# Chunked attention and a feed-forward layer on one core: eight zero products in the front's waits, and the second batch's first keys loaded and interleaved at other steps

## The chip, the cores and the metric

The kernel runs on one core of one Trainium2 chip. The metric is the device time of one execution in microseconds (us), given as a median over runs; the profile is one further execution with the hardware profiler on. TensorE (PE) multiplies, VectorE (DVE), ScalarE (ACT) and GpSimd (POOL) do the rest, and transfers (DMAs) are issued from the queues of SyncE (SP) and GpSimd. PEld stands for TensorE's weight loads, which overlap its products. The granted clock (PEclk) is the share of its full clock that TensorE was given.

## The reference

Four batches, 8 heads of width 64, 768 tokens, eight memory keys and values a head. Each chunk of 32 queries sees the memory, 16 keys to the left of the chunk, the chunk, and 8 to the right; then comes a normalised feed-forward layer with a residual:

```python
for c in range(nc):                      # 24 chunks of 32
    l_start = max(0, c * 32 - 16); r_end = min(S, c * 32 + 32 + 8)
    q_c = q[:, :, c * 32 : c * 32 + 32]
    k_full = np.concatenate([mem_k, k[:, :, l_start:r_end]], axis=2)
    v_full = np.concatenate([mem_v, v[:, :, l_start:r_end]], axis=2)
    scores = scale * np.matmul(q_c, k_full.transpose(0, 1, 3, 2))
    a = softmax(scores)
    out[:, :, c * 32 : c * 32 + 32] = np.matmul(a, v_full)
x = out.transpose(0, 2, 1, 3).reshape(B, S, H * D)
xn = (x - mu) / np.sqrt(var + 1e-06) * g_ln
return x + np.maximum(xn @ w_ch1, 0.0) @ w_ch2      # 512 -> 2048 -> 512
```

## The kernel before

The 3072 tokens are 24 tiles of 128, six to a batch. A tile's attention is: scores (`qk`, products at line 316), their maximum and difference on VectorE (lines 325 and 328), the exponential on ScalarE (line 338), the weights turned through TensorE and copied (`pt`, lines 348 and 353), the product with the values (`val`, line 362), division and row sum on VectorE (`tokens`, lines 371 to 378), and the subtraction of the mean (`shift`, on ScalarE at line 389 for the first tiles and on GpSimd at line 385 later). `turn_x` turns the result through TensorE (line 414) and copies it (line 420). `root` squares it on ScalarE (line 400) and takes the power on GpSimd (lines 404 and 408).

The feed-forward layer works on pairs of tiles, `u` from 0 to 11. `up` makes two blocks of 128 hidden columns (line 452) and `relu` copies them (line 443). From pair 1 on `down7` makes the way back as seven block products instead of eight (line 528), from sums of blocks made on VectorE (`r_sum` line 522, `w2_sum` line 507), and adds each product to the residual (line 535).

Keys and queries of a batch come in two halves. `load_octets` issues two DMAs for a half from GpSimd's queue (line 111). For batch 0 `turn_k`, `turn_q` and `turn_v` turn them as they land (products at line 214, copies at lines 227 and 235). For later batches `mix` first copies a half into another order, two heads beside each other (line 246, on VectorE for the keys, on ScalarE for the queries), and `later_k` and `later_q` turn that (line 255). The values of later batches come head by head, two DMAs each (`load_v_head`, lines 120 and 125), also from GpSimd's queue, and `v_shared` copies shared rows within on-chip memory (line 142).

The order on each engine is the order of the program text: the schedule is written by hand, and each engine works through its queue strictly in that order, an instruction that waits holding all behind it. There are two parts.

- The front (to line 817) is a straight list of calls: the first tiles' attention, the first pairs, and the loads of both weight matrices. `warm(n, p)` (line 595) puts n products of 128x512 zeros on TensorE (line 599); their result goes to a bank that is overwritten later. The front uses them where TensorE waits for a transfer or a copy.
- From `u = 2` on a table `plan` says which calls are made at which of a pair's 17 steps: `at(u, step, fn, ...)` appends to a step's list; at even steps `up` follows the list, at odd steps `down7` of the pair before. Calls of one step run in the order in which they were entered.

For batch 2 (`b = 2`, so `u0 = 3`) the first halves of keys and queries belong to pair-step `w = 2`, which has steps of its own: keys loaded at step 5, queries at step 9, keys interleaved at step 10. At the same pair-step the table has, in this order, V loads at steps 0, 2 and 4, `qk` of tiles 6 and 7 at step 4, `val` of tile 6 at step 9, `val` of tile 7 at step 11, `turn_x` of tile 6 and `qk` of tile 8 at step 12, `root` of tile 6 at step 13, `turn_x` of tile 7 at step 14, and `qk` of tile 9 at step 15. `later_k` of the first half comes at step 1 of pair-step 3.

Of the kernel before, what the change touches and what calls it, by code (L numbers as in the profile page):

```python
# [16 lines left out]
def kernel(  # L17
# [43 lines left out]
    V = [sb.tile([128, NG, H, VW], FP16, name=f"V{i}") for i in range(2)]  # L61
# [26 lines left out]
    def slot():  # L88
        banks["turn"] += 1
        return banks["list"][banks["turn"] % len(banks["list"])]  # L90

    def use(*b):
        banks["list"], banks["turn"] = list(b), -1
# [4 lines left out]
    def free(ap, off, pattern, parts=None):  # L98

        p = list(ap.ap[0]) if parts is None else [ap.ap[0][0], parts]  # L100
        return bass.AP(tensor=ap.tensor, offset=ap.offset + off, ap=[p] + [list(x) for x in pattern])
# [103 lines left out]
    def copy_on(engine):  # L205
        return nc.scalar.copy if engine == "A" else nc.vector.tensor_copy

    def turn(src, jj, n, p=None):

        p = slot() if p is None else p  # L210
        pv = as16(p)
        for r in range(8):
            for par in range(2):
                nc.tensor.matmul(
                    out=pv[64 * par : 64 * par + 64, 2 * n * r : 2 * n * r + 2 * n],
                    lhsT=src[0 : 2 * n, 2 * jj + par, r, :],
                    rhs=identity[0 : 2 * n, 0 : 2 * n],
                    is_transpose=True, start=True, stop=True,
                    tile_position=(0, 64 * par),
                )  # L220
        return pv
# [10 lines left out]
    def to_rows(b, pv, jj, engine, n, oct0, lo=0, hi=None):  # L232

        hi = n if hi is None else hi
        copy_on(engine)(
            out=free(QD[b % 2], 2 * jj * S + 8 * (oct0 + lo), [[S, 2], [8, hi - lo], [1, 8]]),
            in_=free(pv, 2 * lo, [[1, 2], [2, hi - lo], [2 * n, 8]]),
        )
# [29 lines left out]
    def turn_k(b, half, jj, engine):  # L268
        to_stream(KT[b % 2], turn(raw[0][half], jj, 48), jj, engine, 48, 48 * half)
# [35 lines left out]
    def qk_products(t, p=None):  # L305
        b, tt = t // 6, t % 6
        p = slot() if p is None else p
        for y in range(2):
            for j in range(4):
                for gg in range(2):  # L310
                    g = 2 * tt + gg
                    for par in range(2):
                        rows, col = slice(64 * par, 64 * par + 64), 64 * gg + 32 * par
                        q0 = 64 * g + 32 * y
                        k0 = BLK * g + 32 * y
                        nc.tensor.matmul(  # L316
                            out=p[col : col + 32, 128 * j + 64 * y : 128 * j + 64 * y + 64],
                            lhsT=QD[b % 2][rows, j, q0 : q0 + 32],
                            rhs=KT[b % 2][rows, j, k0 : k0 + 64],
                            start=True, stop=True, tile_position=(64 * par, col),  # L320
                        )
        return p.rearrange("p (c k) -> p c k", c=8)

    def row_max(t, scores):
        nc.vector.tensor_reduce(out=nmx[t % 2], in_=scores, axis=AX.X, op=ALU.max)  # L325

    def less_max(t, scores):
        nc.vector.tensor_tensor(  # L328
            out=sub[t % 2].rearrange("p (c k) -> p c k", c=8), in0=scores,
            in1=free(nmx[t % 2], 0, [[1, 8], [0, 64]]), op=ALU.subtract,  # L330
        )

    def below_max(t, scores):
        row_max(t, scores)
        less_max(t, scores)
# [260 lines left out]
    def warm(n, p=upb[1]):  # L596

        for _ in range(n):
            nc.tensor.matmul(  # L599
                out=p, lhsT=zeros[:, 0:128], rhs=zeros, start=True, stop=True,  # L600
            )
# [29 lines left out]
    idle = two[:, 512:1024]  # L631
# [7 lines left out]
    nc.vector.memset(VT[:, :, KC - 8 : KC], 0.0)  # L639
    nc.vector.memset(V[0][0:16, 0, :, 64:VW], 0.0)  # L640
    nc.vector.memset(mhalf, -0.5)
    warm(4, idle)
    for j in range(2):
        turn_k(0, 0, j, "VA"[j])
    warm(1, idle)
    q0 = [turn(raw[1][0], j, 32, one[j]) for j in range(2)]
    for lo in (0, 16):
        for j in range(2):
            to_rows(0, q0[j], j, "VA"[j], 32, 0, lo, lo + 16)
    s0 = qk_products(0, two[:, 0:512])  # L650
    s1 = qk_products(1, dnb[0])
    below_max(0, s0)
    use(upb[0], upb[1])
    turn_v(0, 0, "A")
    weights(0)
    turn_v(0, 1, "V")
    row_max(1, s1)
    warm(2, idle)
    use(dnb[1], one[0], upb[0], upb[1])
    v_turn(0, "V")  # L660
    v_turn(1, "V")
# [159 lines left out]
    def at(u, step, fn, *args):  # L821
        plan.setdefault((u, step), []).append((fn, args))
# [33 lines left out]
    for b in range(2, B):  # L856
        u0 = 3 * b - 3
        for half in range(2):
            w = u0 - 1 + half
            at(w, 5 if w == 2 else 1, load_octets, 0, half, k, b, 48 * half, 48)  # L860
            at(w, 9 if w == 2 else 3, load_octets, 1, half, q, b, 48 * half, 48)
            at(w, 10 if w == 2 else 12, mix, 0, half, "V")
            at(w + 1, 5, mix, 1, half, "A")
            for n, step in enumerate((1, 6, 11, 15)):
                if n < 2:
                    at(w + 1, step, later_k, b, half, n, "V")
                else:
                    at(w + 1, step, later_q, b, half, n - 2, "A")
            for n, step in enumerate((0, 2, 4, 12, 13, 14, 15, 16)):
                at(w, step, load_v_head, b, 4 * half + n // 2, n % 2)  # L870
        at(u0 + 1, 0, load_v_ends, b)
        at(u0 + 1, 6, v_shared, b, 0, NG)
        at(u0 + 1, 6, v_mem, b)
        at(u0, 14, mem_cols, KT[b % 2], memKT[:, 4 * b : 4 * b + 4, :], True)
# [58 lines left out]
```

## Time and profile before

| what | us |
|---|---|
| median of 3 runs (lowest, highest) | 232.98 (232.91, 233.85) |
| the profiled execution | 233.83 |
| its span | 232.1 |
| TensorE busy in the span | 218.9 (94%) |
| VectorE busy | 162.8 (70%) |
| ScalarE busy | 124.6 (54%) |
| GpSimd busy | 115.6 (50%) |

The page of the profile gives each engine's busy time and the span in 40 slices of 5.8 us, in tenths. A row of instructions in order of time has: start, duration, engine, line, operation, output <- inputs, shape, count (xN when several were merged), and in brackets the idle time ahead of it and what ended it. A row of the chain of work has start, duration, and what the end of the execution hung on at that time. Matmuls are pipelined, so records of neighbouring products overlap a little, and the duration of one includes the time until its result stands.

### The profile page before, as it was taken

What the parts mean: (1) busy time and instruction counts of PE and PEld (TensorE: products, weight loads), DVE (VectorE), ACT (ScalarE), POOL (GpSimd) and SP (SyncE); (2) the same over time, 40 slices, a digit from 0 to 9 for tenths busy, and PEclk for the clock granted to TensorE, in tenths of its full rate; (3) what the DMA queues carried; (4) which work ended last, traced back from release to release, by engine and by line L of the source; (5) the groups of instructions that cost most, each with busy time, mean ns of one, the idle gap of its engine ahead of it and who ended that gap; (6) DMA issues with size and microseconds to landing.
All of it is one profiled execution on the core that took longest, in us unless ns stands there. A gap on an engine that the chain in (4) does not pass through costs nothing.

```text
span 232.1 us, 8538 instructions
## 1 busy us (share of the span) xinstructions
PE 218.9 (94%) x3712; PEld 190.6 (82%) x3712; DVE 162.8 (70%) x380; ACT 124.6 (54%) x237; POOL 115.6 (50%) x197
## 2 busy tenths in 40 slices
PE   7699987999998799999999999999999999999993
PEld 3556876876896789999989998999999999899982
DVE  4657665588995997797577796895684875646372
ACT  2243673979461748739646458558437265444310
POOL 7869998589943595912724945613031121220000
PEclk9959999999999999999999999999999999999999
DMA  5999999999898399783781991943102002011022
GB/s 79 189 205 205 215 213 200 187 76 60 76 176 120 101 76 143 123 98 45 141 114 14 151 160 51 111 81 76 45 6 85 8 3 90 3 48 45 1 93 92
DMA packets 43282, 23.25 MB, mean 100 GB/s; under 512 B 29884, under 2 KB 39676, under 8 KB 43172
## 3 DMA queue, kind: packets, MB, share of 16 engines
q0 software_dynamic: 38320, 14.48, 52.1%
q1 hardware_dynamic: 4924, 8.22, 12.6%
q8 instruction: 29, 0.48, 0.8%
q14 instruction: 9, 0.07, 0.1%
HBM read 29.02 MB, written 6.29 MB: 152 GB/s over the span
## 4 chain that ended last, share of the span: by engine, by line
PE 81%; DMA 6%; DVE 4%; POOL 3%; issue 2%; ACT 2%; POOLq 0%; DVEq 0%
PE upb L452 32%; PE dnb L528 26%; PE two L362 3%; DMA raw<-in_k_dram 3%; PE one L255 3%; PE dnb L477 3%; PE one L414 3%; DMA raw<-in_v_dram 2%; PE one L316 2%; PE one L348 2%; POOL raw L111 2%; ACT rT L443 1%; DVE xs L372 1%; PE one L599 1%; DVE KT L227 1%
## 5 line engine op out<-in xcount | busy, mean ns | idle before, releaser
L452 PE MATMUL upb<-xT,w1c 128*128 128x256 f16 x736 | 94.7, 273 | 1.0 <-ACT rT L443 0.7
L452 PEld LDWEIGHTS <-w1c 128*128 128x128 f16 x736 | 77.9, 114 | 2.8 <-DVE xT L420 0.8
L443 ACT ACTIVATE rT<-upb 128x512 f16<-128x512 f32 x92 | 53.6, 595 | 36.6 <-PE upb L452 34.8
L535 DVE SCALAR_TENSOR_TENSOR xs<-dnb,rstd,xs 128x256 f32<-128x256 f32 x77 | 36.9, 479 | 27.0 <-PE dnb L528 26.6
L528 PEld LDWEIGHTS <-RS 128*128 128x128 f16 x352 | 33.8, 98 | 3.7 <-issue 0.2
L338 ACT ACTIVATE P<-sub 128x512 f16<-128x512 f32 x24 | 15.2, 634 | 39.1 <-DVE sub L328 39.1
L528 PE MATMUL dnb<-T,RS 128*128 128x256 f16 x264 | 33.9, 273 | 0.0
L385 POOL TENSOR_SCALAR xn<-xs,nmean 128x512 f16<-128x512 f32 x18 | 12.8, 710 | 38.3 <-PE upb L452 20.5
L528 PEld LDWEIGHTS <-rT 128*128 128x128 f16 x264 | 25.1, 98 | 2.5
L404 POOL TENSOR_SCALAR veps<-ssq 128x1 f32<-128x1 f32 x24 | 5.0, 207 | 44.7 <-ACT sq L400 44.3
L528 PE MATMUL dnb<-w2c,rT 128*128 128x256 f16 x176 | 22.7, 273 | 0.0
L522 DVE TENSOR_TENSOR RS<-rT 128x1024 f16<-128x1024 f16 (+2 forms) x23 | 15.2, 662 | 9.2 <-ACT rT L443 9.2
L120 POOL DMA_DIRECT2D V<-in_v_dram x24 | 20.9, 871 | 1.0 <-PE dnb L528 0.7
L400 ACT ACTIVATE sq<-xs,nmean 128x512 f16<-128x512 f32 x24 | 17.3, 721 | 0.1
L372 DVE CUSTOM_DVE_ANT_1 xs<-two,rec 128x512 f32<-128x512 f32 x24 | 16.6, 691 | 0.8
L408 POOL TENSOR_TENSOR rstd<-veps,mhalf 128x1 f32<-128x1 f32 x24 | 15.0, 625 | 2.0
L328 DVE TENSOR_TENSOR sub<-one,nmx 128x512 f32<-128x512 f32 x22 | 15.2, 691 | 0.8
L325 DVE TENSOR_REDUCE nmx<-one 128x8 f32<-128x512 f32 x22 | 15.0, 683 | 0.8 <-PE one L316 0.8
L125 POOL DMA_DIRECT2D V<-in_v_dram x24 | 15.5, 647 | 0.0
L353 ACT COPY PT<-one 128x512 f16<-128x512 f16 x21 | 12.2, 588 | 5.6 <-PE one L348 5.6
L420 DVE COPY xT<-one 128x512 f16<-128x512 f16 x21 | 8.8, 418 | 4.7 <-PE one L414 4.6
L255 PEld LDWEIGHTS <-raw 96*128 96x128 f16 x192 | 10.6, 97 | 1.7 <-issue 0.5
(115 smaller groups left out, 314.3 us busy)
## 6 DMA issues: line engine op xcount, KB each, us to landing
out_dram<-xs SPq DMA_DIRECT2D x23, 256.0 KB, 2.0
raw<-in_k_dram POOLq DMA_DIRECT2D x16, 192.0 KB, 5.5
raw<-in_q_dram POOLq DMA_DIRECT2D x12, 192.0 KB, 6.0
w1c<-in_moe_w_ch_dram POOLq DMA_DIRECT2D x4, 512.0 KB, 8.4
w2c<-in_moe_w_ch_dram POOLq DMA_DIRECT2D x4, 512.0 KB, 11.0
V<-in_v_dram POOLq DMA_DIRECT2D x24, 77.0 KB, 3.9
V<-V SPq DMA_DIRECT2D x3, 360.0 KB
V<-in_v_dram POOLq DMA_DIRECT2D x24, 44.0 KB, 3.2
```

The costliest lines, as they stand in the source:

```text
L120: nc.gpsimd.dma_start(out=V[b % 2][72:128, 0 : NG - 1, h, 0:64], in_=dram(v, base + 16 * D, [[64, 56], [64 * 64, NG - 1], [1, 64]]),)
L125: nc.gpsimd.dma_start(out=V[b % 2][0:32, 1:NG, h, 0:64], in_=dram(v, base + 48 * D, [[64, 32], [64 * 64, NG - 1], [1, 64]]),)
L255: nc.tensor.matmul(out=pv[:, 96 * r : 96 * r + 96], lhsT=mixed[i][0:96, jj, r, :], rhs=identity[0:96, 0:96], is_transpose=True, start=True ...
L328: nc.vector.tensor_tensor(out=sub[t % 2].rearrange("p (c k) -> p c k", c=8), in0=scores, in1=free(nmx[t % 2], 0, [[1, 8], [0, 64]]), op=AL ...
L338: nc.scalar.activation(out=P[t % 3], in_=sub[t % 2], func=ACTF.Exp, scale=0.125)
L372: nc.vector.tensor_tensor_reduce(out=x.rearrange("p (h d) -> p h d", h=H), in0=free(two, 0, [[128, 8], [1, 64]]), in1=free(r, 0, [[1, 8], ...
L400: nc.scalar.activation(out=sq, in_=xs[t % 9], func=ACTF.Square, bias=nmean[t % 6], scale=1.0, accum_out=ssq[i],)
L443: nc.scalar.activation(out=o, in_=i, func=ACTF.Relu)
L452: nc.tensor.matmul(out=p[:, 256 * hb : 256 * hb + 256], lhsT=free(w1c[hc // 4][:, dt, :], hc % 4, [[4, 128]]), rhs=xT[u % 3][:, dt, :], st ...
L522: nc.vector.tensor_tensor(out=RS[k][:, lo:hi, :], in0=a[:, lo:hi, :], in1=b[:, lo:hi, :], op=op)
L528: nc.tensor.matmul(out=p[:, 0:256], lhsT=left[:, n, :], rhs=right(n), start=(n == 0 and not add), stop=(n == 7), skip_group_check=add,)
L535: nc.vector.scalar_tensor_tensor(out=x, in0=p[:, 0:256], scalar=rstd[t % 9], in1=x, op0=ALU.mult, op1=ALU.add,)
```

## The change

Five places in the front get more zero products, eight in all: 4 to 6 before `turn_k` of the first keys, 1 to 2 before the first queries are turned, one before the scores of tile 0, three behind the scores of tile 1 and ahead of the first values, and 2 to 3 before the first turned values. In the plan, for `w == 2` alone, the two DMAs of the keys go from step 5 to step 3, and `mix` of the keys from step 10 to step 14. On GpSimd's queue the two DMAs so come ahead of the V load of step 4. In VectorE's queue `mix` comes behind the tokens of tile 7, the copy of tile 6's turned tokens, maximum and difference of tile 8, a sum of `down7`, and the copy of tile 7's turned tokens. The step of the queries' load isn't altered, nor is any other pair-step.

```diff
     nc.vector.memset(mhalf, -0.5)
-    warm(4, idle)
+    warm(6, idle)
     for j in range(2):
         turn_k(0, 0, j, "VA"[j])
-    warm(1, idle)
+    warm(2, idle)
     q0 = [turn(raw[1][0], j, 32, one[j]) for j in range(2)]
     for lo in (0, 16):
         for j in range(2):
             to_rows(0, q0[j], j, "VA"[j], 32, 0, lo, lo + 16)
+    warm(1, idle)
     s0 = qk_products(0, two[:, 0:512])
     s1 = qk_products(1, dnb[0])
+    warm(3, idle)
     below_max(0, s0)
     use(upb[0], upb[1])
     turn_v(0, 0, "A")
     weights(0)
     turn_v(0, 1, "V")
     row_max(1, s1)
-    warm(2, idle)
+    warm(3, idle)
...
         for half in range(2):
             w = u0 - 1 + half
-            at(w, 5 if w == 2 else 1, load_octets, 0, half, k, b, 48 * half, 48)
+            at(w, 3 if w == 2 else 1, load_octets, 0, half, k, b, 48 * half, 48)
             at(w, 9 if w == 2 else 3, load_octets, 1, half, q, b, 48 * half, 48)
-            at(w, 10 if w == 2 else 12, mix, 0, half, "V")
+            at(w, 14 if w == 2 else 12, mix, 0, half, "V")
             at(w + 1, 5, mix, 1, half, "A")
```

## The prediction

> **What bounds the kernel now.** I read the page first, then tables of busy time by stage, then the instructions in order of time on TensorE (PE) and VectorE (DVE) around the edited places, then the chain that ended last.
>
> ```profile
> PE 218.9 (94%) x3712; PEld 190.6 (82%) x3712; DVE 162.8 (70%) x380; ACT 124.6 (54%) x237; POOL 115.6 (50%) x197
> PE   7699987999998799999999999999999999999993
> PEclk9959999999999999999999999999999999999999
> ```
>
> The first row says that TensorE is the bound: 94% of the span. The slices show where it isn't at its best: the front, where one slice has half the clock, and the 13th and 14th slices (70 to 81 us), where it idles. The change edits exactly these two stages, so I priced each from its own rows.
>
> ```profile
> 7.65:11.06 3.41, 2.08 (x110) 1.55 (x111) 2.57 (x6) 1.50 (x4) 2.54 (x6) 1.00 1.14 182
> 11.06:14.47 3.41, 3.06 (x48) 1.84 (x42) 2.62 (x7) 1.39 (x3) 1.57 (x5) 0.50 1.24 206
> 14.47:17.89 3.42, 3.42 (x56) 1.98 (x57) 1.35 (x4) 1.12 (x2) 3.38 (x6) 0.50 1.24 204
> 4.23:7.65 3.42, 2.71 (x70) 1.84 (x69) 1.89 (x12) 0.01 (x1) 3.42 (x7) 1.00 1.21 192
> 11.00:11.50 0.50, 0.50 (x24) 0.50 (x20) 0.31 (x1) 0.04 (x1) 0.50 (x2) 0.56 1.26 211
> 17.50:18.00 0.50, 0.50 (x3) 0.19 (x2) 0.50 (x2) 0.00 (x0) 0.46 (x2) 0.61 1.25 205
> ```
>
> Columns: stretch, length, busy of PE, PEld, DVE, ACT, POOL, then the granted clock. In 11.00:11.50 the mean 0.56 puts the fall from 1 to 0.5 at 11.06; in 17.50:18.00 the mean 0.61 puts the return at 17.89. The clock was half for 6.83 us. In the 3.41 us ahead of the fall TensorE was busy 2.08 (61%); in the 3.42 before those, 2.71 (79%), and the clock stayed.
>
> **Part A, eight zero products.** Each is a 128x512 product on zeros into a half of `two` that nobody reads before it is overwritten. They go 4 to 6 before the keys, 1 to 2 before the queries, none to 1 before the first scores, none to 3 before the values, 2 to 3 before the turned values.
>
> ```profile
> 5.09 1.04 PE L599 MATMUL two<-zeros 128*128 128x512 f16 x4
> 6.74 0.87 PE L214 MATMUL dnb<-identity,raw 96*64 96x96 f16 x32 [0.61 <-DMA raw<-in_k_dram]
> 7.54 0.39 PE L599 MATMUL two<-zeros 128*128 128x512 f16 x1
> 8.31 0.69 PE L214 MATMUL one<-identity,raw 64*64 64x64 f16 x32 [0.38 <-DMA raw<-in_q_dram]
> 9.27 0.55 PE L316 MATMUL two<-KT,QD 64*32 64x64 f16 x32 [0.26 <-DVE QD L235]
> 10.78 1.28 PE L214 MATMUL upb<-identity,raw 96*64 96x96 f16 x32 [0.69 <-DMA raw<-in_v_dram]
> 11.99 1.04 PE L599 MATMUL two<-zeros 128*128 128x512 f16 x2
> 16.44 0.63 PE L362 MATMUL two<-V,PT 64*32 64x65 f16 x32
> 19.17 0.39 PE L414 MATMUL one<-identity,xn 128*128 128x128 f16 x4
> 31.75 0.41 PE L285 MATMUL one<-identity,KT 128*64 128x128 f16 x8
> ```
>
> Four products in 1.04 make at most 0.26 each at full clock. The waits they fill: two (0.52) in 0.61; one (0.26) in 0.38; one in 0.26; three (0.78) in 0.69, so at most 0.09 late. The cover is each time the transfer or the copy named in the row's bracket; were it earlier, a product would cost its 0.26. The fifth place is priced in the walk below. Busy time in 7.65:11.06 rises by five products, 1.30, to some 3.3 of 3.41, well over the 79% at which the clock held. So I take it that the clock holds.
>
> What that is worth is a walk along the path, with these rows for the other engines:
>
> ```profile
> 12.10 1.02 DVE L227 COPY KT<-upb 128x192 f16<-128x192 f16 x2 [0.79 <-PE upb L214]
> 15.02 0.59 ACT L353 COPY PT<-one 128x512 f16<-128x512 f16 x1 [2.17 <-PE one L348]
> ```
>
> The values still land by 10.78. Their 32 products take 0.87 instead of 1.28, so the DVE copies run from about 11.75 (12.10) to 12.77. The three zero products end by 12.4 and hide under those copies. Two turned groups at 0.41 follow, to about 13.4, then the turned weights, 0.4 (four 128x128 products, as many as at 19.17), to 13.8, and their copy on ACT, 0.59, to 14.4 (15.61 before). Meanwhile the next two groups and a zero product fill TensorE, and the value products run 14.45 to 14.9, where they ended at 17.07: 2.2 earlier. Normalising, shifting and the turn at 19.17 hang on these by DVE and ACT work whose length the clock doesn't alter, so the turn comes at about 17.0.
>
> Bounds of A: at best half of the busy time at half clock, (3.06 + 3.42) / 2 = 3.2; at worst the clock falls anyway, the three products before the turned values take 0.52 each at half rate (two took 1.04), and 0.52 + 0.09 = 0.6 is lost. I take 2.1, near the walk, because of what is late next:
>
> ```profile
> 23.03 0.64 PE L214 MATMUL two<-identity,raw 128*64 128x128 f16 x16 [0.20 <-DVE xT L420]
> L111 POOL DMA_DIRECT2D raw<-in_q_dram x2: 657/660/663, 8.2 to 8.8; - x2
> DMA to landing us min/median/max: 10.5/11.1/11.9
> 25.32 5.38 POOL L434 TENSOR_SCALAR w1c<-w1c,g_col 128x512 f16<-128x512 f16 x8 [0.20 <-DMA w1c<-in_moe_w_ch_dram]
> 30.53 0.80 PEld L452 LDWEIGHTS <-w1c 128*128 128x128 f16 x8
> 46.08 0.19 POOL L404 TENSOR_SCALAR veps<-ssq 128x1 f32<-128x1 f32 x1 [0.27 <-ACT sq L400]
> ```
>
> The second part of the queries lands at 8.8 + 11.9 = 20.7 at the latest and would be wanted at 23.03 - 2.2 = 20.8. The third block of weights is scaled by 25.32 + 5.38 / 2 = 28.0 and wanted at 28.3. Both fit, but barely, so a gain over 2.3 would be cut there. POOL waited for ACT at 46.08, so it moves up too.
>
> [...]
>
> **Part B, load and interleaving of batch 2's first keys.** `load_octets` goes from step 5 to 3 of pair-step u=2: its two DMAs pass one V load on POOL. `mix` goes from step 10 to 14 in DVE's queue, past the tokens of tile 7, the copy of turned tile 6 and the softmax head of tile 8.
>
> ```profile
> 64.49 0.84 POOL L120 DMA_DIRECT2D V<-in_v_dram  x1
> 65.33 1.17 POOL L111 DMA_DIRECT2D raw<-in_k_dram  x2
> 65.91 7.22 DMA raw<-in_k_dram
> 70.62 0.42 PE L362 MATMUL two<-V,PT 64*32 64x65 f16 x32
> 73.42 1.04 PE L528 MATMUL dnb<-T,rT 128*128 128x256 f16 x8
> 73.22 0.76 DVE L246 COPY raw<-raw 96x1024 f16<-96x1024 f16 x2 [2.80 <-DMA raw<-in_k_dram]
> 73.90 0.20 DVE L371 RECIPROCAL rec<-two 128x8 f32<-128x8 f32 x1
> 75.94 0.40 PE L414 MATMUL one<-identity,xn 128*128 128x128 f16 x4 [1.48 <-POOL xn L385]
> 77.10 0.63 ACT L338 ACTIVATE P<-sub 128x512 f16<-128x512 f32 x1 [5.78 <-DVE sub L328]
> 77.70 0.68 DVE L325 TENSOR_REDUCE nmx<-one 128x8 f32<-128x512 f32 x1
> 78.27 1.03 PE L452 MATMUL upb<-xT,w1c 128*128 128x256 f16 x8 [0.71 <-ACT rT L443]
> 79.43 0.69 DVE L522 TENSOR_TENSOR RS<-rT 128x1024 f16<-128x1024 f16 x1 [0.32 <-ACT rT L443]
> 79.50:91.50 12.00, 11.63 (x237) 10.47 (x234) 11.60 (x26) 8.03 (x16) 10.41 (x18) 1.00 1.01 99
> ```
>
> Here the stall is read off: the keys are issued at 65.33, land 7.22 after the second issue, at 73.13; DVE stands 2.80 for them, and behind it the tokens of tile 7 (73.90), though their products ended at 71.04. Through POOL's shift that stops TensorE for 1.48, and through the late weights on ACT for another 0.71: 2.19.
>
> After the change the tokens start at 71.05, 2.85 sooner. The sum added at the end of step 13 must wait for the products that end at 74.46 (0.3 lost), the interleaving now takes its 0.68 (73.22 to 73.90) in between, and the scores of tile 9 end on TensorE at about 75.95 (0.15 lost): the maximum at 77.70 starts 2.85 - 0.3 - 0.68 - 0.15 = 1.7 sooner. The 0.32 that DVE then waited for ACT goes too, as ACT has its weights early: 2.0 to 2.1. From there DVE is full (11.60 of 12.00), so it, not TensorE's 2.19, sets the gain: 2.1. Bounds: 2.80 at best, DVE's whole wait; 1.4 if the 0.68 is paid again in the full stretch. The keys pass one V load (0.84), so they land by 72.3, and are wanted at about 75.1: 2.8 of cover. The V load goes 1.17 later and is collected only two pair-steps on.
>
> **The sum.** The profiled execution took 233.83, span 232.1 and 1.73 around it; it stands 0.85 over the median of 232.98, at the slow end of the three runs. Its half-clock stretch may be why; the forecast removes that stretch, so I subtract from 233.83: 233.83 - 2.1 - 2.1 = 229.6.
>
> **The rivals.** (1) *The clock falls all the same.* For: the busy share of TensorE isn't all there is to it, as 11.06:14.47 was busy 3.06 of 3.41 and the clock did not come back. Against: the products are the same kind that held it in 4.23:7.65. A costs 0.6 or less, B stays: 233.83 + 0.6 - 2.1 = 232.3; from the median, 231.5. [...] (2) *DVE eats half of B.* For: 11.60 of 12.00 busy. Against: it stood 2.80 just before. The 0.68 is paid again: 230.3. (3) *The interleaving stays the bound, so B does nothing:* the time is 231.7. Against: the tokens overtake it in the same queue. (4) *Slower: the keys land late at the new place,* and with `mix` stand the maximum of tile 9 and the sums for the next pair. It costs one for one past 75.1; 0.5% over the median, 234.2, needs 4.6 on top of 229.6, a landing at 79.7, which is 14.6 after an issue of the second part at about 65.1. The slowest landing quoted is 11.9.
>
> **How the numbers follow.** Chances: forecast 0.63 (228.6 to 230.2), rival 1 0.13, rival 2 0.16, rival 3 0.04, rival 4 0.04. I take 0.5%, 1.2 us, as what a measurement here tells from no change, and count it from the median. Faster: forecast, rival 2, half of 1 and of 3: 0.87; same: the other halves and a little: 0.09; slower: 0.04. Low end 228.6: A at 2.6 and B at 2.6, toward their upper bounds. High end 231.8: it takes in rivals 2 and 3 and half of 1.
>
> **What would show it.** A: PEclk at 1.00 in all of 7 to 18 us, the turn of tile 0's tokens at about 17.0, no row of zero products over 0.3 each. B: no wait of DVE on the interleaving, keys landing by 72.3 minus A's gain, TensorE's waits of 1.48 and 0.71 gone, and DVE the next bound at 80 to 90 us. The prediction is wrong if the clock still drops, or if the time gained at 19 us is not there at 60.

## The result and the profile after

The changed kernel took 232.06 us (median of 21 runs, 230.95 to 234.67) against 233.85 for the kernel before (21 runs, 232.65 to 235.39). The ratio is 0.9942, with a 95% interval of 0.9915 to 0.9969: faster by 0.6%, where 229.6 and a range of 228.6 to 231.8 were forecast. The ratio leaves out two slow runs of the changed kernel; the means of the rest give the same 0.9942, the medians of all 0.9923. The profiled execution took 231.75, its span 230.0. From the page of the changed kernel:

```profile
PE 218.4 (95%) x3720; PEld 190.0 (83%) x3720; DVE 162.1 (70%) x380; ACT 124.6 (54%) x237; POOL 115.4 (50%) x197
PE   7979787999999989999999999999999999999993
PEclk9999999999999999999999999999999999999999
q8 instruction: 29, 0.48, 0.8%
```

The granted clock no longer falls (1.00 in all of 7 to 18 us, 0.69 in the mean before) and the hole at 70 to 81 us is filled, as both parts were to do. But a front at full clock didn't bring the front's end forward. TensorE's instructions of the changed kernel in order of time:

```profile
6.78 0.87 PE L214 MATMUL dnb<-identity,raw 96*64 96x96 f16 x32
10.79 0.87 PE L214 MATMUL upb<-identity,raw 96*64 96x96 f16 x32
12.37 0.81 PE L599 MATMUL two<-zeros 128*128 128x512 f16 x3 [0.71 <-DVE sub L328]
14.38 0.41 PE L285 MATMUL one<-identity,KT 128*64 128x128 f16 x8 [0.78 <-issue]
18.38 0.40 PE L414 MATMUL one<-identity,xn 128*128 128x128 f16 x4 [0.17 <-ACT xn L389]
26.47 0.33 PE L316 MATMUL one<-KT,QD 64*32 64x64 f16 x20 [1.41 <-issue]
38.54 0.38 PE L452 MATMUL upb<-xT,w1c 128*128 128x256 f16 x2 [1.37 <-issue]
49.41 1.03 PE L477 MATMUL dnb<-w2c,rT 128*128 128x512 f16 x4
76.61 1.06 PE L452 MATMUL upb<-xT,w1c 128*128 128x256 f16 x8
84.24 0.50 PE L255 MATMUL one<-identity,raw 96*128 96x96 f16 x8 [0.64 <-DVE sub L328]
```

and those of the kernel before that answer to them and were not shown:

```profile
14.38 0.61 PE L348 MATMUL one<-identity,P 128*128 128x128 f16 x4 [0.35 <-issue]
25.93 0.27 PE L316 MATMUL one<-KT,QD 64*32 64x64 f16 x12 [0.20 <-issue]
38.25 0.25 PE L285 MATMUL dnb<-identity,KT 128*64 128x128 f16 x2 [1.17 <-issue]
48.63 1.03 PE L477 MATMUL dnb<-w2c,rT 128*128 128x512 f16 x4
85.58 0.50 PE L255 MATMUL one<-identity,raw 96*128 96x96 f16 x8 [0.37 <-DVE sub L328]
121.88 0.30 PE L316 MATMUL one<-KT,QD 64*32 64x64 f16 x16 [0.34 <-issue]
```

The turn at 19.17 came at 18.38, 0.8 sooner. The first product of pair 0's way back (L477), where the front ends, came 0.78 *later*. From there to the second turn of interleaved keys (L255) it took 34.83 instead of 36.95: part B gave 2.12. The rest of the difference of 2.1 in the spans, some 0.75, came behind 113 us, the row at 121.88 being one of the short waits that were gone there; that this rest belongs to part B is not shown. VectorE interleaves the keys (L246) and takes the maximum of tile 9 (L325) in the changed kernel at

```profile
76.01 0.75 DVE L246 COPY raw<-raw 96x1024 f16<-96x1024 f16 x2
76.76 0.69 DVE L325 TENSOR_REDUCE nmx<-one 128x8 f32<-128x512 f32 x1
```

What ate the front are the waits marked "issue", in which the profile shows nothing that TensorE waited for. The second and third fall in the middle of a group of equal products, the first between two groups. The three together grew from 1.72 to 3.56, by 1.84, nearly as much as the full clock was to give. How many products had begun by then is the count behind PE in a table of busy time from 0 to just before and just after each wait. The kernel before:

```profile
0.00:14.10 14.10, 10.73 (x222) 6.01 (x222) 8.38 (x25) 4.18 (x8) 10.15 (x23) 0.89 0.91 146
0.00:25.70 25.70, 21.74 (x476) 13.83 (x476) 15.15 (x41) 9.08 (x16) 21.37 (x41) 0.87 1.06 173
0.00:37.10 37.10, 32.25 (x730) 22.83 (x731) 22.56 (x59) 17.68 (x33) 32.37 (x58) 0.91 1.07 185
```

The changed kernel:

```profile
0.00:13.60 13.60, 11.40 (x222) 5.99 (x222) 7.48 (x23) 4.28 (x8) 10.58 (x24) 1.00 0.92 145
0.00:25.20 25.20, 21.59 (x476) 13.30 (x476) 14.95 (x42) 9.28 (x16) 21.07 (x41) 1.00 1.07 173
0.00:37.20 37.20, 31.63 (x730) 22.01 (x731) 22.38 (x59) 17.47 (x32) 32.66 (x58) 1.00 1.08 186
```

The counts are the same, 222, 476 and 730, 254 apart, though the eight added products put other work there. The waits end at 14.38, 25.93 and 38.25 before and at 14.38, 26.47 and 38.54 after. So the theory after the result: TensorE ran out of *instructions*. 254 products are 508 instructions, a weight load and a product each (the expectations below put them at about 512), and the waits behind such blocks end 11.55 and 12.32 us apart before, 12.09 and 12.07 after.

The trace shows what may be the supply itself. The row of queue q8 above, marked "instruction", counts packets of 0.02 MB, and narrow windows place each. In the changed kernel one falls in 24.0 to 24.5:

```profile
q8 instruction: 1, 0.02, 11.7%
```

In steps of 0.1 the first five fall at 11.9, 18.0, 24.1, 30.1 and 36.1 in the changed kernel, and at 11.9, 18.0, 23.6, 29.9 and 36.0 in the kernel before. Each of the three waits ends 2.2 to 2.5 behind the first, third and fifth. There are 26 such waits ahead of TensorE's products in the first 60 us of this case's twelve profiles; the eight whose packets are placed to 0.1, the six here and two of the last experiment below, each end 2.2 to 2.5 behind one. Why TensorE seldom waits behind the second and fourth is not shown.

The rivals were that the loss at 49 us came from part B, that the stalls belong to places in the work, and that a wait which part A had added ate its gain.

### The profile page after: what moved, and what is told of

Its sections match the earlier page's. It is cut to its first block, busy times and chain, and to the rows that moved or that the text cites. A ratio compares the mean times of both kernels' runs of the same rounds, so it can differ in the third digit from the quotient of the medians.

```text
span 230.0 us, 8554 instructions
## 1 busy us (share of the span) xinstructions
PE 218.4 (95%) x3720; PEld 190.0 (83%) x3720; DVE 162.1 (70%) x380; ACT 124.6 (54%) x237; POOL 115.4 (50%) x197
## 4 chain that ended last, share of the span: by engine, by line
PE 86%; DVE 6%; issue 3%; ACT 2%; POOL 1%; DVEq 0%; POOLq 0%
PE upb L452 34%; PE dnb L528 28%; PE two L362 4%; PE one L255 3%; PE dnb L477 3%; PE one L316 3%; PE one L414 2%; PE two L599 2%; PE one L348 2%; POOL raw L111 1%; DVE sub L328 1%; DVE xs L372 1%; DVE KT L227 1%; DVE nmx L325 1%; ACT rT L443 1%
## 5 line engine op out<-in xcount | busy, mean ns | idle before, releaser
L325 DVE TENSOR_REDUCE nmx<-one 128x8 f32<-128x512 f32 x22 | 15.1, 685 | 1.2 <-PE one L316 1.2
L255 PEld LDWEIGHTS <-raw 96*128 96x128 f16 x192 | 10.6, 97 | 2.0 <-issue 0.8
L420 DVE COPY xT<-one 128x512 f16<-128x512 f16 x21 | 8.8, 420 | 4.5 <-PE one L414 4.1
```

What stands on the lines that cost most here:

```text
L255: nc.tensor.matmul(out=pv[:, 96 * r : 96 * r + 96], lhsT=mixed[i][0:96, jj, r, :], rhs=identity[0:96, 0:96], is_transpose=True, start=True ...
```

## The experiments

**Part A alone.**

```diff
-            at(w, 3 if w == 2 else 1, load_octets, 0, half, k, b, 48 * half, 48)
+            at(w, 5 if w == 2 else 1, load_octets, 0, half, k, b, 48 * half, 48)
-            at(w, 14 if w == 2 else 12, mix, 0, half, "V")
+            at(w, 10 if w == 2 else 12, mix, 0, half, "V")
```

> Part A alone: the eight zero products, with the loading and interleaving of batch 2's keys as before. Theory 1 (TensorE's instructions are delivered at a limited rate in the front, about 512 per 12.1 us between the stalls that end at 14.4, 26.5 and 38.5 us in the changed kernel, so that what the full clock gains by 19 us is given back by 50): the product that started at 48.63 before starts at 49.0 to 49.6, the stall at 74 to 78 us is there, and the time is 233.0 to 234.8, no gain. Theory 2 (the loss at 50 us comes from part B or is chance): the product starts at about 47 and the time is about 231.7.

Measured: 233.95 (12 runs) against 233.41, ratio 1.0016 (0.9983 to 1.0048). Part A is worth nothing that can be measured. Nor does a gain show among runs of high clock alone: the eight with a mean granted clock of 0.996 or more have a median of 233.85, such runs of the kernel before 233.07. Rows of its profile:

```profile
5.44 2.74 PE L599 MATMUL two<-zeros 128*128 128x512 f16 x6
8.11 1.25 PE L214 MATMUL dnb<-identity,raw 96*64 96x96 f16 x32
50.04 1.03 PE L477 MATMUL dnb<-w2c,rT 128*128 128x512 f16 x4
```

In this execution the six zero products took 0.46 each, half the rate of the changed kernel (0.25 each), and the keys' turn began at 8.11, not 6.78: the cover that the prediction gave them (0.61) was gone. With four zero products, also at half rate, it began at 7.26 (part B alone, next), so the two more cost 0.85 there.

**Part B alone.**

```diff
-            at(w, 5 if w == 2 else 1, load_octets, 0, half, k, b, 48 * half, 48)
+            at(w, 3 if w == 2 else 1, load_octets, 0, half, k, b, 48 * half, 48)
-            at(w, 10 if w == 2 else 12, mix, 0, half, "V")
+            at(w, 14 if w == 2 else 12, mix, 0, half, "V")
```

> Part B alone: batch 2's keys loaded at step 3 and interleaved at step 14, no added zero products. Theory 1: all of the change's gain is here: 2.1 us, 231.5 to 232.0 at a median of before of 233.85, and the stretch of half clock in the front stays. Theory 2 (part B gives half and part A the other half): about 232.9.

Measured: 231.87 (12 runs), ratio 0.9923 (0.9895 to 0.9952). All of the change's gain is here, 0.8% or 1.8 us. Rows of its profile:

```profile
7.26 1.49 PE L214 MATMUL dnb<-identity,raw 96*64 96x96 f16 x32
26.90 0.27 PE L316 MATMUL one<-KT,QD 64*32 64x64 f16 x12 [1.50 <-issue]
49.32 1.03 PE L477 MATMUL dnb<-w2c,rT 128*128 128x512 f16 x4
```

Other than expected, the granted clock shows no half stretch. The lengths of the products do: the keys took 1.49 where they take 0.87 in the changed kernel, and the last two zero products, begun at 13.04 and 13.4, some 0.62 each where they take 0.38, so TensorE ran at about half rate to nearly 14 us. The front is that of the kernel before, which was slow at another time, yet L477 starts at 49.32 where it started at 48.63: two executions of one front lie 0.7 apart. So the 0.78 of the changed kernel's profile isn't clear of that by itself. What is clear is that no gain of 2 us shows: the front that was at full rate from 5.3 us on ends at 49.41, those that were slow for 6.8 and some 8 us at 48.63 and 49.32.

**More instructions, no more columns.** Two of the three zero products ahead of the values become 32 small ones.

```diff
-    warm(3, idle)
+    warm(1, idle)
+    small(32, idle)       # 64x32 weights, 64 columns each
     below_max(0, s0)
```

> The changed kernel with two of the three zero products ahead of the first values replaced by 32 small ones (64 rows, 32 columns of weights, 64 columns), which take no longer on TensorE (32 value products of that kind take 0.35 us) but are 60 instructions more. Theory 1 (limited delivery of instructions): the three stalls stay at the same counts of products from the start, 222, 476 and 730, so each falls 30 products earlier in the work, and the product that starts at 49.41 in the changed kernel starts up to 60 / 512 x 12.1 = 1.4 us later, about 50.8; the time is 0.7 to 1.5 us over the changed kernel. Theory 2 (the stalls belong to places in the work, that is to data or semaphores): they stay at the same places of the work, the product starts at 49.4, and the time is that of the changed kernel.

Measured: 235.18 (10 runs), ratio 1.0061 (1.003 to 1.0092), where the changed kernel had 0.9942: some 2.8 us for work that streams no longer. TensorE in its profile:

```profile
15.09 0.64 PE L214 MATMUL upb<-identity,raw 96*64 96x96 f16 x19 [2.51 <-issue]
28.76 0.58 PE L316 MATMUL one<-KT,QD 64*32 64x64 f16 x50 [0.40 <-issue]
34.62 0.38 PE L285 MATMUL one<-identity,KT 128*64 128x128 f16 x7 [1.08 <-issue]
```

The first stall is again at 222 products, which now is in the turn of the values (19 of its 32 are left), 30 products earlier in the work; the second is at 476, with 50 of 64 score products left where 20 were. The third was expected at 730 and came at 603, which is 127 behind the second: half a block of 254, one packet further, and none shows at 730. The stalls here go by the count, in steps of 127. The loss is larger than expected (2.8 against 1.5 at most, and L477 starts at 53.02, not at 50.8; part A alone, whose keys began at the same 8.11, has 50.04). The clock fell as well behind the long stall (0.84 in 11.6 to 17.4, 0.87 in 17.4 to 23.2), and all ten runs have a mean clock of 0.993 or less, so the size isn't that of the instructions alone:

```profile
PEclk9988997999999999999999999999999999999999
```

**Fewer instructions, the same columns.** Two steps of the first pair run once at full width in place of twice at half width.

```diff
-    for s in range(2, 4):
-        up_half(s, 0, four[s])          # 16 products of 128 columns each
+    up_full(2, four[2])                 # 8 products of 256 columns
...
     for s in range(4):
-        up_half(s, 1, four[s], "A")
+        # s = 0, 1 as before; s = 3: up_full(3, four[3]); relu of 2 and 3 here
```

> The changed kernel with the half-width products of two steps of the first pair (32 of 128 columns) put together to 16 of 256 columns: the same columns streamed, 32 instructions fewer. Theory 1: the stalls stay at the counts 222, 476 and 730, the work behind them is up to 32 / 512 x 12.1 = 0.75 us earlier at 50 us, and the time is 0.4 to 0.8 us under the changed kernel. Theory 2: no change at 50 us, or some tenths later since one block waits longer for its place; the time is within 0.3 us of the changed kernel.

Measured: 230.95 (10 runs), ratio 0.9892 (0.9861 to 0.9924). It is faster than the kernel before; against the changed kernel the two intervals (0.9861 to 0.9924 and 0.9915 to 0.9969) just touch. Its stalls:

```profile
27.01 0.27 PE L316 MATMUL one<-KT,QD 64*32 64x64 f16 x12 [1.34 <-issue]
39.17 0.41 PE L316 MATMUL one<-KT,QD 64*32 64x64 f16 x30 [0.49 <-issue]
48.73 1.03 PE L488 MATMUL dnb<-w2c,rT 128*128 128x512 f16 x4
```

Same counts (476 and 730), and more work done by each. L488 is line 477 of the other kernels.

**The same without part A.** Part B and the merged products, no added zero products.

```diff
-    warm(6, idle)
+    warm(4, idle)
...                                      # and so at the four other places
```

> Part B alone, with two steps of the first pair at full width (16 products, 32 instructions fewer), and no added zero products: 24 products fewer than in the changed kernel by 50 us. Theory 1 (the front is bound by the delivery of TensorE's instructions, one block of 254 products from one stall to the next in about 12.05 us): faster than part B alone by 16 / 254 x 12.05 = 0.75 us, about 231.1, and as fast as or up to 0.4 us faster than the changed kernel with the same merging (230.95). Theory 2 (the zero products are worth something by the clock): slower than that kernel by 0.4 to 1 us, 231.4 to 232.

Measured: 230.81 (6 runs), ratio 0.9872 (0.9828 to 0.9917), as good as with part A, and 1.3% faster than the kernel before. Its profiled execution happened to have a half clock in the front, and yet its front ended earliest of all:

```profile
PEclk9958999999999999999999999999999999999998
14.60 0.61 PE L348 MATMUL one<-identity,P 128*128 128x128 f16 x4 [0.90 <-issue]
47.50 1.03 PE L488 MATMUL dnb<-w2c,rT 128*128 128x512 f16 x4
```

That is the plainest row against part A's reasoning. The products at half rate only filled time that was otherwise spent waiting at 476, where this execution shows no stall at all. Over many runs a lower clock does go with a longer time. Of 35 runs of the kernel before, the 19 with a mean clock of 0.996 or more had a median of 233.07, the 16 with less 233.69, 0.6 apart; in the two other groups of 17 runs of that kernel they lie 1.2 and 1.1 apart. Where in the span the clock fell in those runs is not on record.

**Six zero products fewer.**

```diff
-    warm(3, one[1])
+    warm(1, one[1])
-    warm(4, one[1])
+    warm(2, one[1])
-    warm(2, one[1])
     turn_x(1, two[:, 0:512])
```

> As the kernel of part B with merged products, less six of the zero products that stand between the first value products and the second turned keys. Theory 1: six products fewer are worth 6 / 254 x 12.05 = 0.28 us, about 0.3 under the kernel it is made from, unless the clock falls. Theory 2 (these products hold the clock, and the clock sets the front's time): a half clock from about 18 us and 0.5 to 2 us slower.

Measured: 230.78 (10 runs), ratio 0.9879 (0.9842 to 0.9916): no difference to the kernel it is made from. In its profile the products run at full rate from 14 us on, so the second theory finds no support, and the 0.3 of the first is under what these runs can tell.

**Second half of batch 0's keys with half as many products.**

```diff
     v_copy(3, v3, "V")
+    mix(0, 1, "V")
-    turn_k(0, 1, 0, "V")
+    later_k(0, 1, 0, "V")
-    turn_k(0, 1, 1, "A")
+    later_k(0, 1, 1, "A")
```

> As the kernel of part B with merged products, with the second half of batch 0's keys interleaved on VectorE first (two copies, 0.76 us, in a wait of VectorE at about 19 us) and turned two heads at a time: 16 products instead of 32, 32 instructions fewer. Theory 1: up to 0.75 us faster than the kernel it is made from, less if the stalls behind it are used up by then (0.5 us was left at the third in the merged kernel). Theory 2: no gain, or 0.5 us lost to the copies.

Measured: 230.9 (4 runs), ratio 0.9868 (0.9816 to 0.9919): no gain that shows. TensorE waited 0.83 for a copy of turned tokens (L420) behind the new copies on VectorE, and 0.61 at the third stall; the merged kernel had little stall left to win.

**The added wait on the scores.** In the changed kernel the maximum of tile 0's scores, which lie in the same tile as the zero products' target, waited for three of these. VectorE there:

```profile
10.90 0.69 DVE L325 TENSOR_REDUCE nmx<-two 128x8 f32<-128x512 f32 x1 [1.34 <-PE two L599]
```

It started at 9.89 before. The change added this wait, and the prediction did not see it. The experiment takes it away by another bank:

```diff
-    warm(3, idle)
+    warm(3, dnb[1])
     below_max(0, s0)
...
-    warm(3, idle)
+    warm(3, dnb[1])
     use(dnb[1], one[0], upb[0], upb[1])
```

> The changed kernel with the six zero products around the first values written to a bank that nobody reads then, in place of the second half of the tile that holds tile 0's scores. In the changed kernel the maximum of those scores waited for three zero products (it started at 10.90, 9.89 before), and the next three waited 0.71 for the difference. Theory 1 (delivery of instructions is the bound there): the maximum starts at about 9.9 and the second wait is gone, but the stall still ends at about 14.4 at a count of 222 products, the first block product of pair 0's way back stays at about 49.4, and the time is within 0.3 us of the changed kernel. Theory 2 (the added wait on the scores ate part A's gain): the product starts 0.7 to 1.5 us earlier and the time falls by as much.

Measured: 231.85 (12 runs), ratio 0.9938 (0.9903 to 0.9973), as the changed kernel. In its profile:

```profile
10.16 0.69 DVE L325 TENSOR_REDUCE nmx<-two 128x8 f32<-128x512 f32 x1 [0.35 <-PE two L316]
14.49 0.41 PE L285 MATMUL one<-identity,KT 128*64 128x128 f16 x8 [1.15 <-issue]
26.58 0.33 PE L316 MATMUL one<-KT,QD 64*32 64x64 f16 x20 [1.41 <-issue]
38.65 0.38 PE L452 MATMUL upb<-xT,w1c 128*128 128x256 f16 x2 [1.37 <-issue]
```

The maximum no longer waits for zero products, TensorE comes to product 222 earlier, and waits there longer (1.15, not 0.78) for nearly the same moment; L477 starts at 49.52. The added wait was real and cost nothing.

**What makes a block late.** The loads of the second weight matrix are moved to leave a quiet stretch. First on the merged kernel:

```diff
-    for c in range(2):
-        load_w2(c)
...
-    for c in range(2, 4):
-        load_w2(c)
...
     load_octets(0, 0, k, 1, 0, 48)
+    for c in range(4):
+        load_w2(c)
```

> As the kernel of part B with merged products, with the four loads of the second weight matrix moved behind the first keys of batch 1 on GpSimd's queue, from 21 to 25 us to about 32 us. It asks what makes a block of instructions late. Theory 1a (the fetch waits its turn among the data transfers, which hold over half of the transfer engines' time there): the block from 222 to 476 products takes less than 12 us, its stall (1.3 to 1.5 us) shrinks to under 0.5 and the next block, fetched amid the moved loads, stays slow. Theory 1b (a fetch takes its time whatever else moves): the blocks stay at 12.0 us. The whole time can go either way, as the second matrix is wanted at about 49 us.

Measured: 237.9 (4 runs), ratio 1.0151 (1.0092 to 1.0211), and no stall at 476 or 730. But the kernel it is made from hardly had them either (none and 0.15), so its stalls tell nothing. Then the same edit on the changed kernel:

> The changed kernel itself with the four loads of the second weight matrix moved behind the first keys of batch 1, so that hardly anything is transferred between 26 and 32 us. In the changed kernel the third stall, at a count of 730 products, is 1.37 and ends 12.07 after the second. Theory 1a (the blocks of instructions are late because they wait among the data transfers): the third stall falls under 0.4, as its block is fetched in the quiet stretch; the second, whose block is fetched while the queues are still full, stays at 1 us or more. Theory 1b (a fetch takes its time whatever else moves): both stay at 1.4. The whole time will be longer, since the values of batch 1 and the second matrix then come late.

One run: 236.28 beside 233.44 for the kernel before. Its stalls, and a row of busy time by stretch, whose last two columns are the transfer engines' share and the GB/s that they moved:

```profile
14.86 0.41 PE L285 MATMUL one<-identity,KT 128*64 128x128 f16 x8 [0.78 <-issue]
26.94 0.33 PE L316 MATMUL one<-KT,QD 64*32 64x64 f16 x20 [1.41 <-issue]
26.00:32.00 6.00, 4.46 (x108) 3.94 (x109) 3.93 (x8) 4.13 (x9) 5.15 (x8) 1.00 0.11 18
```

The first two stalls are those of the changed kernel to the hundredth (0.78 and 1.41). The third, 1.37 there, is gone; the stretch ahead of it moved 18 GB/s, where the changed kernel moved

```profile
26.00:32.00 6.00, 4.93 (x112) 4.42 (x113) 3.69 (x7) 4.34 (x9) 6.00 (x10) 1.00 1.09 216
```

The instruction packets agree. The first and third of this profile fall at 12.4 and 24.6, 2.5 and 2.3 ahead of the ends of its two stalls. Behind the one at 24.6 they fall at 28.0 and 33.2, 3.4 and 5.2 apart, where the changed kernel has 6.0 and 6.0. So the third block was late beside 216 GB/s of data and not beside 18; these are one execution of each kernel, and what holds the packet up on its way is not shown. The kernel as a whole loses by the move: the transfers of the second matrix are 6% of the chain of work that ended last, some 14 us.

## Why the prediction was wrong

- **Zero products fit the waits of the front.** Right for the profiled pair: keys, queries, first scores and values began at 6.78, 8.32, 9.28 and 10.79 (before: 6.74, 8.31, 9.27, 10.78). Wrong as a general cover: in the execution of part A alone, six products at half rate delayed the keys to 8.11, 0.85 more than four did.
- **The clock holds.** Right in the changed kernel's profile: 1.00 in all of 7 to 18 us. Not in every run: of the 19 runs behind the ratio, five have a mean clock of 0.992 or 0.993, with a median of 234.09, where the 14 with 0.997 or more have 232.0. Where it fell in the five is not on record, and even the 14 are 2.4 over the forecast.
- **What that is worth, the walk to 2.1.** This is the step that failed. The walk went through data alone. It took the 0.35 at 14.38 for something that would shrink with the rest, and passed over the 1.17 at 38.25, the longest wait in the front behind the first products. The turn of tile 0's tokens came 0.8 sooner, not 2.2, since the first stall ended at 14.38 as before. From there to 38.5 two blocks took 24.2 (before 23.9), and eight products more are 8 / 254 of a block, 0.4 us of work put off. The three waits for instructions took 3.56 instead of 1.72. At the front's end the term was +0.78 in this pair of profiles instead of -2.1, and two executions of one front lie 0.7 apart; over many runs part A alone is 1.0016 (0.9983 to 1.0048), a gain of 0.4 us at most. The measured 232.06 lies where the first rival put it (231.5 to 232.3), but by chance, since in that rival the clock falls.
- **The base of 233.83.** It fits the later median of 233.85, but not for the reason given: the 233.83 was taken as 0.85 over the middle of the runs, and among the 21 it is the middle.
- **What is late next after the clock.** The prediction named the queries' landing and the scaled weights. Neither was, at a gain of 0.8; instructions were. It had said that it would be wrong if the time gained at 19 us weren't there at 60: so it was.
- **A busy TensorE holds the clock.** Not shown. Between 7.65 and 11.06 TensorE's busy time did rise from 2.08 to 3.27 (3.3 was forecast), and the clock stayed. But between 11.06 and 14.47 the changed kernel had TensorE busy for only 1.92 of 3.41, less than the 2.08 (61%) ahead of the fall in the kernel before, with waits of 0.71 and 0.78 where the longest between 5 us and that fall was 0.69, and its clock stayed at 1.00. What the clock goes by no run shows; it wasn't what bounded the front.
- **The interleaving leaves VectorE's path, 2.1.** Right, step by step: 2.12 in the profile, 0.9923 alone. The maximum of tile 9 started at 77.70 and now starts at 76.76, which, counted from the front's end that came 0.78 later, is the 1.7 of the sum. TensorE's waits of 1.48 and 0.71 are gone, and the full stretch on VectorE took back a little (0.64 waited for a difference, 0.37 before), as the sum said.
- **The keys land sooner.** Wrong, without effect. They were issued ahead of the V load and still landed 7.2 to 7.5 later, at 73.3 (before 73.13); the interleaving came at 76.01, so there was cover. What moved the time is the later place in VectorE's queue. The earlier load alone wasn't tried.

## What to carry to other kernels

When an idle stretch in a trace has no releaser and falls within a group of equal instructions, count the instructions up to it in two versions. If the count agrees and the work doesn't, as here at 222, 476 and 730, suspect that the engine waits for its program; here the faster front only waited longer, 3.56 instead of 1.72. Then look for the instruction packets in the view of the transfers: the eight such waits whose packets were placed ended 2.2 to 2.5 behind one. In such a stretch count instructions too, not busy time alone. In this one a wide product did better than two narrow ones of the same columns: merging 32 into 16 took the ratio from 0.9942 to 0.9892 with part A and from 0.9923 to 0.9872 without, intervals that overlap a little each time. A few extra products were too little to measure (eight in part A alone, six in the leaner kernel). In the changed kernel's profile the supply ran short beside data transfers of 207 and 211 GB/s.

## What the runs showed of the hardware

By the count, TensorE's instructions come through the transfer queue q8: 29 packets for the changed kernel's 7440 weight loads and products, an estimate of about 257 to a packet if all of them come that way, and stalls 127 or 254 products apart, which is 254 or 508 instructions. The trace doesn't name the engine of a packet, so this is inferred. Beside 207 and 211 GB/s of data the two stretches between the ends of the changed kernel's three stalls took 12.09 and 12.07 us, and TensorE stood up to 1.41 at their ends.

The granted clock reads 1.00 in the first 5.8 us of the two kernels, of parts A and B alone, and of the kernels with more and with fewer instructions, also where products took double: in part A alone six zero products took 2.74 at 5.44, in the changed kernel

```profile
5.28 1.47 PE L599 MATMUL two<-zeros 128*128 128x512 f16 x6
```

so the rate of the first microseconds is read from the products' length. The zero products were at full rate from 5.09 on in the kernel before (1.04 for four) and from 5.28 in the changed kernel, from 9.29 in part A alone (0.60 for two), and in part B alone only behind those at 13.04 (1.03 for two).
